# Two transformer layers on one core: GELU passes grouped on ScalarE, an earlier weight load, a new hand-made order

## The chip, the cores and the metric

The kernel runs on one core of one Trainium2 chip. A core has five engines with a queue of instructions each: TensorE (PE, matrix products), VectorE (DVE), ScalarE (ACT, table functions such as exp and GELU), GpSimd (POOL) and SyncE (SP, which here only issues DMAs). The engines run independently and wait for each other on semaphores. The metric is the device time in microseconds of one execution; the median over the runs counts.

## The reference

The input x has 2048 rows of 448. Two layers are computed, each an attention block and a mixer block:

```python
x = x + A(layernorm(x))        # attention: 16 heads of 28; softmax(q k^T / sqrt(28)) v, then @ wo
x = x + B(layernorm(x))        # mixer, on y = layernorm(x):
    h  = gelu(layernorm(y) @ w1)           # 448 -> 448
    hs = shift(h) @ w2                     # four quarters of the columns, shifted by +1, -1, +2, -2 rows
    x1 = y + hs
    B  = x1 + gelu(layernorm(x1) @ w3) @ w4   # 448 -> 1792 -> 448
```

Because the mixer shifts rows by up to two, the second half of the mixer for a tile of 128 rows needs the first half of the tile before and of the tile after.

## The kernel before, in words

The 2048 rows are 16 tiles of 128; x stays in SBUF as `x_res` for the whole kernel. Queries are worked off in units: four units of four tiles in layer 0; in layer 1 three units of four tiles and two of two (`UNITS`). Keys come in parts (`PARTS`): tiles 0 to 3, 4 to 7 and 8 to 15. `ORDER` says which unit meets which part first: in layer 0 unit 0 takes its three parts one after the other; in layer 1 units 0 and 1 alternate over the parts, so that unit 0 on the first part is followed by unit 1 on the first part. Sums of an unfinished unit are spilled to DRAM and loaded again (`t_uload`, `t_norm`).

The exponentials are the main stream. A group of two or three PSUM banks of scores (L1415) is turned into `PT` by one exp on ACT (L1458), and `PT` is multiplied with V (L1485). A share of the banks is done on DVE by a polynomial instead (`t_ditem`, L1370 to L1386). When a unit is finished its sums are copied out of PSUM (L1503), normalised, projected (`t_outproj`) and added to `x_res`.

Then the unit's mixer begins (`spawn_mixer`). `t_mixA` does the first half: statistics, `xn`, a DMA transpose, the product with w1, a copy into `hT`, and one GELU pass in place over all of it (L1648). `t_mixB` does the second half for the tiles from the one before the unit to the last but one (the last unit of layer 0 in two parts of two and three tiles): x1, `xn`, transpose, the product with w3, copies into `h2T` (L1779), two GELU passes in place over seven of 14 chunks each (L1791), and the product with w4, which ends in `x_res` (L1799). After that the next layer can take the tile: statistics, `xn` (L1052), transpose, projections to `kT`, `qT` and `vaug`. The last unit of layer 1 runs a direct variant in the tail, with a GELU per bank.

exp and GELU need different tables on ACT, and each change from one to the other inserts a table load. `GATED[L]` lists the units whose h2T passes wait until the hT pass of the next unit has been issued, so that they run under one table.

Nothing is ordered by hand in the code: every part of the work is a generator, and a planner (`Sched.run`) simulates the five engines with costs written in the code and picks the next instruction again and again. For ACT the key of a candidate is the time from which its inputs are ready; a change of table adds 1.42 us to its planned start. Ties and priorities come from latest start times of an earlier planning round, which `reorder` then shifts by the entries of a long list, `SEEDS`. The result is a fixed program for each engine's queue. When PE would be idle the planner adds filler matmuls (`keep_pe_busy`) on the tile `zero` or `ident`.

The start is in `t_setup`: the first four tiles of x go to `w4` as a staging place, the weights of the projections are loaded, statistics of four tiles are taken, one POOL instruction makes 1/sqrt(variance) for all four (`rstd`, L1156), `xn` follows, and PE transposes and projects. `t_load` issues the loads of the rest of x on POOL's queue. `t_setup2` loads the later weights (wo, w1, w3, w2, w4) once the second unit of layer 0 starts; w1 and w3 need zeroed padding first, which DVE writes (L959).

Of the kernel before, what the change touches and what calls it, by code (L numbers as in the profile page):

```python
# [8 lines left out]
ALU = mybir.AluOpType  # L9
# [168 lines left out]
class Sched:  # L178
# [174 lines left out]
    def run(self):  # L353
        P = self.P
        while True:
# [77 lines left out]
            for k, (t, choice) in enumerate(cand_list):  # L433
# [18 lines left out]
                key = (ready if eng == "act" else max(start, self.cur[eng] + self.EPS) if eng in ("pe", "dve") else start, ranks[k])  # L452
# [29 lines left out]
            if dma:  # L482
                self.cur[eng] = start + 0.1
                t_end = start + kw.get("dma_time", 3.0)
            else:
                self.cur[eng] = max(self.cur[eng], t_end)
# [109 lines left out]
def build_kernel(nc, A_x, A_wqkv, A_wo, B_x, B_w1, B_w2, B_w3, B_w4, out, n_layers=2):  # L596
# [156 lines left out]
    with st:  # L753
# [77 lines left out]
        def bi(b):  # L831
            return int(b[1:])
# [1109 lines left out]
```

## Time and profile before

| | |
|---|---|
| median of 3 runs | 1076.27 us (1075.23 to 1077.58) |
| the profiled execution: its own time, and its span | 1077.48 us, 1075.4 us |
| mean granted TensorE clock | 0.994 |
| first exp on ACT | 31.20 us |
| ACT table loads | 40 |
| exps on ACT (L1458) | 775, 881.2 us busy |
| matmuls on PE | 14185 |

The span is the time from the first to the last instruction of the profiled execution; its own time is a little longer. Times in the profile count from the span's start. Busy time is a sum over one engine; matmuls overlap, so that a busy PE is not PE at its peak. "L1458" is line 1458 of the kernel, and an arrow `out<-in` names the tiles of an instruction. "Idle before, releaser" says how long an engine stood still before an instruction and whose result it then got.

### The profile page before, as it was taken

To read this page: it belongs to the slowest core of one execution; us is meant where nothing else is said; L and a number is where in the kernel's file an instruction comes from. 1 tells how busy PE (TensorE), PEld (TensorE's weight loads), DVE (VectorE), ACT (ScalarE), POOL (GpSimd) and SP (SyncE) were. 2 spreads that over 40 slices of the span, in tenths; PEclk is the share of its full clock that TensorE was granted. 3 is DMA by queue.
4 is the path that set the end of the run, shared out by engine and by line. 5 is a ranking of instruction groups with operands and counts; after the bars stand their busy time and mean duration, and the time that the engine had idled before them with its cause. 6 is when DMAs were issued, how large, how long until landed. Compare 5 with 4: busy or idle time off the path is not lost.

```text
span 1075.4 us, 31722 instructions
## 1 busy us (share of the span) xinstructions
PE 985.7 (92%) x14185; PEld 385.1 (36%) x14188; DVE 840.6 (78%) x1855; ACT 1025.4 (95%) x924; POOL 157.1 (15%) x174
## 2 busy tenths in 40 slices
PE   5999999899999988998998999899899899999898
PEld 2333333233333333333334433333333334343455
DVE  6999999699996775756697678999998768645463
ACT  5999999799999999999999998999999999999975
POOL 4220101120111002012123012001020111110101
PEclk9999999799999999999999999999999999999999
DMA  7232105203000001000212312001111010010000
GB/s 199 60 90 63 42 2 137 55 2 36 1 21 22 1 21 22 21 7 16 61 51 66 80 46 76 21 21 41 27 15 37 2 34 12 22 39 12 20 11 23
DMA packets 77104, 41.27 MB, mean 38 GB/s; under 512 B 61288, under 2 KB 70376, under 8 KB 76968
## 3 DMA queue, kind: packets, MB, share of 16 engines
q1 hardware_dynamic: 74856, 35.58, 13.9%
q0 software_dynamic: 2112, 3.67, 1.4%
q8 instruction: 111, 1.82, 0.7%
q14 instruction: 25, 0.20, 0.1%
HBM read 14.20 MB, written 8.13 MB: 21 GB/s over the span
## 4 chain that ended last, share of the span: by engine, by line
ACT 77%; PE 18%; DVE 2%; DMA 2%; issue 1%; POOL 0%; SPq 0%; ACTq 0%; DVEq 0%
ACT PT L1458 67%; PE ps L174 8%; ACT h2T L1791 4%; PE ps L1415 4%; PE ps L1485 3%; ACT L1458 2%; DMA xT<-xn 1%; ACT hT L1648 1%; ACT L1791 1%; PE ps L1796 1%; ACT L1648 1%; PE ps L1770 1%; PE ps L1059 1%; DVE xn L1052 0%; DMA wv<-in_A_wqkv_dram 0%
## 5 line engine op out<-in xcount | busy, mean ns | idle before, releaser
L1458 ACT ACTIVATE PT<-ps 128x1536 bf16<-128x1536 f32 (+1 forms) x775 | 881.2, 1259 | 15.7 <-PE ps L1415 14.2
L1415 PE MATMUL ps<-qT,kT 32*128 32x512 bf16 (+1 forms) x2184 | 304.7, 360 | 38.5 <-ACT PT L1458 34.1
L1485 PE MATMUL ps<-PT,vaug 128*32 128x512 bf16 (+1 forms) x2184 | 232.8, 362 | 6.1 <-ACT PT L1458 4.5
L1415 PEld LDWEIGHTS ps<-qT,kT 32*128 32x128 bf16 x2184 | 76.0, 91 | 261.2 <-ACT PT L1458 149.9
L174 PE MATMUL ps<-xT,w 128*32 128x512 bf16 (+3 forms) x2412 | 159.4, 350 | 4.2 <-DMA xT<-xn 2.7
L1779 DVE CAST h2T<-ps 128x512 bf16<-128x512 f32 (+2 forms) x126 | 73.6, 584 | 37.4 <-PE ps L174 33.9
L1485 PEld LDWEIGHTS ps<-PT,vaug 128*32 128x32 bf16 x2184 | 60.6, 94 | 112.8 <-issue 52.4
L174 PE MATMUL ps<-w,h2T 128*32 128x448 bf16 x1476 | 85.9, 354 | 5.4 <-ACT h2T L1791 5.1
L1370 DVE TENSOR_SCALAR dT<-ps 128x512 f32<-128x512 f32 x116 | 79.2, 684 | 13.3 <-PE ps L1366 12.1
L174 PE MATMUL ps<-wk_pad,zero 128*32 128x256 bf16 x1796 | 84.6, 277 | 0.0
L1386 DVE SCALAR_TENSOR_TENSOR dT<-dU,dT 128x512 int32<-128x512 f32 x116 | 79.9, 689 | 0.8
L1381 DVE SCALAR_TENSOR_TENSOR dU<-dF 128x512 f32<-128x512 uint16 x116 | 79.7, 687 | 1.0
L1383 DVE SCALAR_TENSOR_TENSOR dU<-dF,dU 128x512 f32<-128x512 uint16 x116 | 79.3, 684 | 0.9
L174 PEld LDWEIGHTS ps<-xT,w 128*32 128x32 bf16 x2412 | 56.8, 95 | 62.4 <-issue 34.7
L1082 POOL TENSOR_TENSOR sq<-qT 128x512 bf16<-128x512 bf16 (+1 forms) x32 | 31.3, 985 | 264.5 <-DVE qT L1068 190.8
L1799 DVE SCALAR_TENSOR_TENSOR x_res<-x_res,mst,ps 128x448 f32<-128x448 f32 x32 | 21.5, 677 | 55.4 <-PE ps L174 44.3
L1738 POOL TENSOR_TENSOR x_res<-x_res,x1b 128x448 f32<-128x448 f32 x32 | 37.0, 1164 | 156.1 <-DVE x1b L1719 155.2
L174 PEld LDWEIGHTS ps<-wk_pad,zero 128*32 128x32 bf16 x1796 | 45.2, 96 | 24.3 <-issue 18.7
L1082 POOL TENSOR_TENSOR sq<-kT 128x512 bf16<-128x512 bf16 (+1 forms) x32 | 31.3, 980 | 130.6 <-DVE kT L1068 91.7
L174 PEld LDWEIGHTS ps<-w,h2T 128*32 128x32 bf16 x1476 | 36.5, 96 | 38.4 <-issue 10.8
L1376 DVE TENSOR_SCALAR dF<-dT 128x512 uint16<-128x512 uint16 x116 | 48.5, 418 | 0.8
L1791 ACT ACTIVATE h2T<-h2T 128x3584 bf16<-128x3584 bf16 (+2 forms) x18 | 46.9, 2605 | 1.8 <-DVE h2T L1779 1.6
(164 smaller groups left out, 1177.4 us busy)
## 6 DMA issues: line engine op xcount, KB each, us to landing
uscr<-u_sb SPq DMA_DIRECT2D x24, 256.0 KB, 2.0
uin<-uscr SPq DMA_DIRECT2D x24, 256.0 KB, 2.7
x_res<-in_A_x_dram POOLq DMA_DIRECT2D x4, 896.0 KB, 7.4
out_dram<-uin SPq DMA_DIRECT2D x16, 112.0 KB, 1.7
w<-in_B_w_dram SPq DMA_DIRECT2D x1, 1568.0 KB, 13.6
w<-in_B_w_dram SPq DMA_DIRECT2D x1, 1344.0 KB, 7.2
h2T<-in_A_wqkv_dram SPq DMA_DIRECT2D x2, 336.0 KB, 4.2
xT<-xn SPq DMA_TRANSPOSE x33, 3.7
```

Of the source, the lines that this page charges most:

```text
L174: return [self.e.matmul(out=out[c:min(c + 32, self.m)], lhsT=lhsT[:, c:min(c + 32, self.m)], rhs=rhs, start=start, stop=stop, tile_positio ...
L1082: yield op("pool", 0.1 + 0.002 * nw, lambda e, si=si: e.tensor_tensor(out=sq[:, si, 0:nw], in0=dst, in1=dst, op=ALU.mult), reads=dkeys, wr ...
L1370: yield op("dve", c_ps(cw), lambda e, b=b: e.tensor_scalar(out=dT[:, s, 0:cw], in0=ps[:, bi(b), 0:cw], scalar1=65536.0 + 127 * 128.0, scal ...
L1376: yield op("dve", c_f2b(cw), lambda e: e.tensor_scalar(out=dF[:, f, 0:cw], in0=dT[:, s, 0:cw].bitcast(U16).rearrange("p (q two) -> p q two ...
L1381: yield op("dve", c_ps(cw), lambda e: e.scalar_tensor_tensor(out=dU[:, v, 0:cw], in0=dF[:, f, 0:cw], scalar=-16384.0, in1=dF[:, f, 0:cw], ...
L1383: yield op("dve", c_ps(cw), lambda e: e.scalar_tensor_tensor(out=dU[:, v, 0:cw], in0=dF[:, f, 0:cw], scalar=EXPD * 16384.0, in1=dU[:, v, 0 ...
L1386: yield op("dve", c_ps(cw), lambda e: e.scalar_tensor_tensor(out=dT[:, s, 0:cw].bitcast(I32), in0=dU[:, v, 0:cw], scalar=EXPC * 2.0 ** -35 ...
L1415: yield op("pe", 0.012 + W / 2400.0, lambda e, bk=bk, r0=32 * j, g=g, kc=kc, q0=q0, W=W, c0=W * h: e.matmul(out=ps[:, bk, c0:c0 + W], lhsT ...
L1458: yield op("act", e_dur(n), lambda e, b0=b0, p0=p0, cnt=cnt, cw=cw: e.activation(out=PT[:, p0:p0 + cnt, 0:cw], in_=ps[:, b0:b0 + cnt, 0:cw ...
L1485: yield op("pe", 0.004 + nt * 0.0133, lambda e, j=j, rhs=rhs, vs=vs, i=i: e.matmul(out=ps[32 * j:32 * j + 32, bi(SUM), 0:128 * nt], lhsT=v ...
L1779: yield op("dve", c_ps(NW), lambda e, fch=fch, b=b: e.tensor_copy(out=h2T[:, fch, hoff:hoff + NW], in_=ps[:, bi(b), 0:NW]), reads=[("ps", ...
L1791: yield op("act", c_act(7 * NW), lambda e, f0=f0: e.activation(out=h2T[:, f0:f0 + 7, hoff:hoff + NW], in_=h2T[:, f0:f0 + 7, hoff:hoff + NW ...
```

## The change

1. In the planner, when ACT holds the GELU table, an exp is compared by its planned start, which includes the change of table, and no longer by the time it is ready. A GELU that is ready before that start goes first.
2. `GATED` of layer 0 becomes (0, 1, 2): the h2T passes of the third unit also wait for the hT pass of the fourth.
3. The zeroing of the padding of w1 and w3 moves from DVE to POOL and to the start (the one of w3 after the scratch use of that tile); the weight loads themselves stay behind the start of the second unit.
4. At the start 100 matmuls on `ident` are put on PE (`t_warm`); the first four tiles' 1/sqrt(variance) is made in two halves; and the loads of the rest of x on POOL wait for the second half.
5. In the planner a DMA issued by POOL now occupies POOL for its planned duration and not for 0.1 us.
6. `SEEDS` is another, shorter list, so that the order of all instructions changes. By the change's own words 20 table loads are left.

```diff
@@ Sched.run
-                key = (ready if eng == "act" else ...
+                key = ((start if self.act_tab == "gelu" and kw.get("tab") == "exp" else ready) if eng == "act" else ...
...
             if dma:
-                self.cur[eng] = start + 0.1
+                self.cur[eng] = start + (dur if eng == "pool" else 0.1)
@@ build_kernel
     SEEDS = [
-        (3033793134, 1, 5, -8.4), (3017015515, 1, 0, -0.6), 570578, 625884, ...
+        (3033793134, 1, 35, -35.9), 510908, 684737, (3033793134, 1, 0, -0.4), ...
     ]
-    GATED = [(0, 1), (0, 1)]
+    GATED = [(0, 1, 2), (0, 1)]
@@ t_setup
+            yield ("spawn", t_warm(), 2)
             yield ("spawn", t_load(ld_x, last), 2)
...
+        def t_warm():
+            b = yield ("acq", ["b3"])
+            for k in range(100):
+                yield op("pe", 0.06, lambda e, b=b: e.matmul(out=ps[:, bi(b), 0:128], lhsT=ident[:, :], rhs=ident[:, :], start=True, stop=True),
+                         reads=[("ident",)], writes=[("ps", bi(b))], touch=[b])
+            yield ("rel", b)
+
         def t_load(ld_x, after):
+            yield ("wait", ("rstd0",))
             for k, c in enumerate([1, 2, 3, 0]):
@@ t_setup2
+            yield op("pool", 0.5, lambda e: e.memset(w1[:, 3, :], 0.0), writes=[("w1z",), ("w1",)], nolk=1)
+            yield ("wait", ("acol",))
+            yield op("pool", 1.9, lambda e: e.memset(w3[:, 3, :], 0.0), writes=[("w3z",), ("w3",)], nolk=1)
             yield ("wait", ("segstart", first_seg[(0, 1)]))
...
-            for (dst, src_, nm, w) in ((w1, B_w1, "w1", 0.3), (w3, B_w3, "w3", 1.0)):
-                yield op("dve", w, lambda e, dst=dst: e.memset(dst[64:128, 3, :], 0.0), writes=[(nm + "z",)])
+            for (dst, src_, nm) in ((w1, B_w1, "w1"), (w3, B_w3, "w3")):
@@ new function, also called by t_ln1
+        def ln_rstd(tiles):
+            sl = slice(tiles[0], tiles[-1] + 1)
+            yield op("dve", 0.1, lambda e: e.tensor_scalar(out=vpe[:, sl], in0=mv[:, sl, 1], scalar1=EPS, scalar2=None, op0=ALU.add), ...)
+            yield op("pool", 0.4 + 0.15 * len(tiles), lambda e: e.tensor_tensor(out=rstd[:, sl], in0=vpe[:, sl], in1=neghalf[:, 0:len(tiles)], op=ALU.pow), ...)
@@ t_ln1
-            for t in tiles:
+            halves = [tiles[:2], tiles[2:]] if L == 0 and c == 0 else [tiles]
+            for part in halves[:-1]:
+                for t in part:
+                    yield from ln_stats(t, True)
+                yield from ln_rstd(part)
+            for t in halves[-1]:
...
+            yield from ln_rstd(halves[-1])
+            if L == 0 and c == 0:
+                yield ("sig", ("rstd0",))
             yield from norm_x(tiles, xs, L == 0 and c == 0)
```

More of the change, by code (lines that the diff above doesn't have):

```diff
@@ L451, in run @@
                         continue
-                key = (ready if eng == "act" else max(start, self.cur[eng] + self.EPS) if eng in ("pe", "dve") else start, ranks[k])
+                key = ((start if self.act_tab == "gelu" and kw.get("tab") == "exp" else ready) if eng == "act" else max(start, self.cur[eng] + self.EPS) if eng in ("pe", "dve") else start, ranks[k])
                 if best is None or key < best[0]:
@@ L970, in ln_stats @@
             yield op("dve", 0.2, lambda e: e.bn_aggr(out=mv[:, t, :], in_=st6[:, t, :]), reads=[("st6", t)], writes=[("mv", t)])
+        def ln_rstd(tiles):
+            sl = slice(tiles[0], tiles[-1] + 1)
+            yield op("dve", 0.1, lambda e: e.tensor_scalar(out=vpe[:, sl], in0=mv[:, sl, 1], scalar1=EPS, scalar2=None, op0=ALU.add),
+                     reads=[("mv", t) for t in tiles], writes=[("vpe", t) for t in tiles])
+            yield op("pool", 0.4 + 0.15 * len(tiles), lambda e: e.tensor_tensor(out=rstd[:, sl], in0=vpe[:, sl], in1=neghalf[:, 0:len(tiles)], op=ALU.pow),
+                     reads=[("vpe", t) for t in tiles] + [("neghalf",)], writes=[("rstd", t) for t in tiles])
         class Slot:
@@ L1152, in t_ln1 @@
             xs = yield from acq_xn(4)
-            sl = slice(t0, t0 + n)
-            yield op("dve", 0.1, lambda e: e.tensor_scalar(out=vpe[:, sl], in0=mv[:, sl, 1], scalar1=EPS, scalar2=None, op0=ALU.add),
-                     reads=[("mv", t) for t in tiles], writes=[("vpe", t) for t in tiles])
-            yield op("pool", 1.0, lambda e: e.tensor_tensor(out=rstd[:, sl], in0=vpe[:, sl], in1=neghalf[:, 0:n], op=ALU.pow),
-                     reads=[("vpe", t) for t in tiles] + [("neghalf",)], writes=[("rstd", t) for t in tiles])
+            yield from ln_rstd(halves[-1])
+            if L == 0 and c == 0:
+                yield ("sig", ("rstd0",))
             yield from norm_x(tiles, xs, L == 0 and c == 0)
```

123 rows, old and new, of the table SEEDS are left out of this document.

## The prediction

> **What bounds the kernel now.** I read the page's busy times and chain first, then the groups of ScalarE (ACT), then a table by stage. Columns of a group: busy us, mean ns of one, then idle before it.
>
> ```profile
> PE 985.7 (92%) x14185; PEld 385.1 (36%) x14188; DVE 840.6 (78%) x1855; ACT 1025.4 (95%) x924; POOL 157.1 (15%) x174
> ...
> ACT 77%; PE 18%; DVE 2%; DMA 2%; issue 1%; POOL 0%; SPq 0%; ACTq 0%; DVEq 0%
> ```
>
> ```profile
> L1458 ACT ACT_TABLE_LOAD x19 | 24.4, 1283 | 0.3
> ...
> L1791 ACT ACT_TABLE_LOAD x12 | 15.4, 1283 | 0.2
> ...
> L1648 ACT ACT_TABLE_LOAD x8 | 10.3, 1283 | 0.1
> ```
>
> ACT is busy 95% of the span and carries 77% of the chain. The three rows are its table loads: 19 back to exp, 20 to GELU; with one at the start, 40. Where is ACT not full? In the next view the fields are the stretch, its length, then busy time of PE, PEld, DVE, ACT, POOL.
>
> ```profile
> 0.00:31.20 31.20, 17.70 (x106) 8.41 (x107) 22.17 (x83) 17.73 (x27) 13.46 (x20) 1.00 0.65 173
> 31.20:186.00 154.80, 145.63 (x1885) 50.09 (x1888) 148.75 (x329) 154.71 (x139) 21.37 (x19) 1.00 0.24 63
> 186.00:216.00 30.00, 25.46 (x258) 7.83 (x251) 20.44 (x38) 23.84 (x22) 4.15 (x4) 0.77 0.35 73
> 216.00:492.00 276.00, 257.42 (x3525) 92.59 (x3527) 214.79 (x441) 275.31 (x233) 35.27 (x36) 1.00 0.09 17
> 492.00:680.00 188.00, 174.04 (x2788) 71.14 (x2780) 145.89 (x324) 179.48 (x152) 36.16 (x40) 1.00 0.22 54
> 680.00:1034.70 354.70, 329.97 (x5211) 131.26 (x5213) 268.31 (x591) 354.07 (x300) 39.38 (x46) 1.00 0.10 24
> 1034.70:1075.40 40.70, 35.45 (x443) 23.81 (x431) 20.28 (x53) 20.27 (x57) 7.27 (x10) 1.00 0.05 16
> ```
>
> ACT idles 13.5 us before the first exp, 6.2 us around 200, 8.5 us between 492 and 680, 20.4 us in the tail after the last exp, and under 1 us in each of the three long stretches: those are ACT's, and what leaves ACT there leaves the time. From 492 to 680 layer 0 hands over to layer 1. How much room PE has is shown by its filler matmuls (tile `zero`), which the planner puts in when PE has nothing to do; PE's own busy time hides that.
>
> ```profile
> 412.00:492.00 80.00, 3.20 (x84) 2.17 (x80) 0.00 (x0) 1.00 0.11 21
> 492.00:680.00 188.00, 6.02 (x132) 3.71 (x132) 0.00 (x0) 1.00 0.22 54
> ```
>
> So in those two stretches PE has 3 to 4% in reserve, and in the second one it shares the bound.
>
> **Part 1, the loads.** One GELU episode of the before, on ACT:
>
> ```profile
> 221.23 94.51 ACT L1458 ACTIVATE PT<-ps 128x1536 bf16<-128x1536 f32 x83
> 315.75 1.28 ACT L1648 ACT_TABLE_LOAD   x1
> 317.05 1.91 ACT L1648 ACTIVATE hT<-hT 112x2048 bf16<-112x2048 bf16 x1
> 318.87 2.43 ACT L1791 ACTIVATE h2T<-h2T 128x2688 bf16<-128x2688 bf16 x1
> ...
> 322.61 1.02 ACT L1458 ACTIVATE PT<-ps 128x1024 bf16<-128x1024 f32 x1
> 323.65 1.28 ACT L1791 ACT_TABLE_LOAD   x1
> 324.94 2.44 ACT L1791 ACTIVATE h2T<-h2T 128x2688 bf16<-128x2688 bf16 x1
> 327.40 1.28 ACT L1458 ACT_TABLE_LOAD   x1
> ```
>
> A single exp stands between the two halves of h2T and costs two loads. With the changed key the planner charges that exp its table switch before it compares, so the second half, ready at once, goes first. Nine pairs exist; one is together already in the tail, eight get rid of two loads each; the third unit of layer 0 joining the fourth's hT pass is two more. That makes 22 by my count; the change says 20, so one more pair of episodes must meet, which can happen where no exp is ready between them. I take 20. Price of one: neighbours under one table overlap (hT ends at 318.96, h2T starts at 318.87, 0.09), across a load they don't, and 0.02 is lost beside it (327.40 + 1.28 to the next): 1.283 + 0.09 + 0.02 = 1.39 us. Twenty are 27.8 us of ACT.
>
> [...]
>
> Ten of the twenty lie in ACT's own stretches (four in 316 to 427, four in 851 to 946, two at 996 to 1009): 13.9 us, full value at best; PE's thin reserve from 412 to 492 can eat the 2.8 us there. The other ten lie in 492 to 680.
>
> **Part 2, the hold.** Unit 2's h2T passes now wait for unit 3's hT pass. On ACT nothing queues behind them, exps pass by. But unit 2 holds tile 7, layer 1's unit 1 has tiles 4 to 7 as queries, and its exps come second in layer 1's order. The rows, DVE and ACT in order of time:
>
> ```profile
> 500.25 3.19 ACT L1791 ACTIVATE h2T<-h2T 128x3584 bf16<-128x3584 bf16 x1
> ...
> 508.39 1.78 DVE L1052 TENSOR_SCALAR xn<-x_res,mv,rstd 128x448 bf16<-128x448 f32 x4 [0.33 <-POOL rstd L1156]
> ...
> 517.96 0.69 DVE L1503 COPY u_sb<-ps 128x512 f32<-128x512 f32 x1
> ...
> 544.15 0.34 DVE L1318 TENSOR_SCALAR qT<-qT,bcol 128x512 bf16<-128x512 bf16 x1
> ...
> 562.42 1.28 ACT L1648 ACT_TABLE_LOAD   x1
> ```
>
> 517.96 is the last copy of layer 0's attention; at 544.49 unit 1's first queries are ready, just in time. In between ACT does layer 1's first unit: 64 banks, two and a half to an exp, 26 exps at 94.51/83 = 1.14 us, 29 us. Now tile 7's GELU waits for the load at 562.42, 44.5 us after the copy, where the queries were due 26.5 us after it. Two delays follow. First, exps run out until hT is ready: 0 to 44.5 - 26.5 = 18 us, as the out-projection and mixer are hurried or not. Second, from the GELU's end to the queries: 41.0 us as it ran (503.44 to 544.49, with slack in it), at the least 6.7 to the end of xn at 510.17, a transpose of 3.7 (page, row below) and about 4 of projection, 14.4. I take 4 and 19, near the low ends, because the planner sees both waits and the low ends are what the work takes; a stall of 23 us, between 14 and 59. Against it the ten loads, 13.9, and some of the old 8.5 us of idle, since PE clears its backlog in the stall: I take 6. Part 2 with its loads: 13.9 + 6 - 23 = -3 us; bounds +8 and -45.
>
> **Part 3, the weights.** The w1 and w3 pads move from DVE, where they queued behind the DVE exps, to POOL at the start; the SP DMAs that followed them can go right behind wo_pad's at 129.29, some 45 us earlier. What they collide with now:
>
> ```profile
> 129.29 2.04 SPq L956 DMA_DIRECT2D wo_pad<-in_A_wo_dram  x4
> ```
>
> ```profile
> xT<-xn SPq DMA_TRANSPOSE x33, 3.7
> ```
>
> ```profile
> 179.39 0.49 SPq L965 DMA_DIRECT2D w<-in_B_w_dram  x1
> ```
>
> ```profile
> 186.41 9.66 DMA xT<-xn
> ```
>
> ```profile
> 199.30 3.28 ACT L1458 ACTIVATE PT<-ps 128x1024 bf16<-128x1024 f32 x3 [3.79 <-PE ps L1415]
> 203.83 4.91 ACT L1458 ACTIVATE PT<-ps 128x1536 bf16<-128x1536 f32 x4 [1.25 <-PE ps L1415]
> 209.79 6.90 ACT L1458 ACTIVATE PT<-ps 128x1536 bf16<-128x1536 f32 x6 [1.05 <-PE ps L1415]
> ```
>
> The last weight load is issued at 179.39, and the transpose at 186.41 takes 9.66 us, not 3.7; PE waits, its clock falls to 0.77 of full in this stretch, ACT loses 3.79 + 1.25 + 1.05 = 6.1 us. Between 0 (another collision) and 6.1; I take 5. POOL's added memsets stand ahead of little; its x loads and squares wait 2 us at most.
>
> **Part 4, the start.** The POOL power behind the x loads, and PE before and after it speeds up:
>
> ```profile
> 7.76 0.17 DVE L1154 TENSOR_SCALAR vpe<-mv 128x4 f32<-128x4 f32 x1
> ...
> 10.90 1.08 POOL L1156 TENSOR_TENSOR rstd<-vpe,neghalf 128x4 f32<-128x4 f32 x1
> ...
> 24.45 1.03 PE L1059 MATMUL ps<-xT,wq_pad 128*128 128x512 bf16 x4
> ...
> 28.78 0.15 DVE L933 TENSOR_SCALAR sc<-sc 128x4 f32<-128x4 f32 x1
> ```
>
> ```profile
> 16.93 4.98 PE ps L1059 x12
> ```
>
> The power is ready at 7.93 and starts at 10.90: 3.0 us go when the x loads wait for it. Twelve projections take 4.98 us cold; at the later rate (1.03 for four) they take 3.1: 1.9 us go if the 100 warm-up matmuls hold. Sum 4.9; I take 5. Low end 0: the bias chain (28.78) also gates the first exp at 31.20 and may not move. High end 9: with that chain moved up too. The x loads themselves land later, but 26 exps cover them.
>
> [...]
>
> **Part 5, the order.** New seeds move everything. The tail's 41 us and the three ACT stretches may change; ACT's idle there is under 1 us each, so there is little to win and something to lose: -2, from 0 to -10 (waits such as the 1.05 and 1.25 above, a handful).
>
> **Sum.** 13.9 - 3 + 5 + 5 - 2 = 19 us off the profiled execution's 1077.48: 1058.5. That execution is 1.2 above the median of 1076.27, so about **1057**.
>
> **Rivals.** (a) Slower: the hold. If hT and the queries keep the pace they ran at, the stall is 18 + 41 = 59, part 2 is -45, the sum -23 or so: **1099**. It decides from a stall of about 42 us on. For it: both delays are in rows, and the extra pair of episodes that meets (Part 1) fits a time without exps. Against it: both paces had slack. (b) PE becomes the bound where loads go: reserve 3.20 of 80 us at 412; half of the 13.9 us is lost and the 6 us of idle stay: **1070**. For it: the filler rows. Against it: ahead of 412 and after 680 filler is plentiful. (c) The start and the weights do nothing (warm-up worn off or in front of the transposes, weights landing on another transpose): **1067**.
>
> **How the numbers follow.** Forecast 0.55, (a) 0.20, (b) 0.13, (c) 0.12. Three runs spread by 0.2%, about 2.2 us, which is what can be told from no change. The forecast itself runs from 1042 (hold at its low end, start 7) to 1068; with (b), (c) and half of (a) the range is 1041 to 1086. Faster: 0.55 + 0.25 less a little where (b) or (c) meets a longer stall, 0.77; same 0.03; slower 0.20.
>
> **What would show it.** Right: 20 loads; ACT's first exp near 26; no 3.8 us wait on ACT near 195, the weights issued near 130; one gap on ACT of 15 to 30 us between layer 1's first and second unit, ended by PE's L1415. Wrong: a gap over 40 us there, the three long stretches with several us of ACT idle, or hT of unit 3 long after the end of layer 1's first unit.

## The result, and the profile after

The changed kernel takes **1081.8 us** (median of 4, 1081.3 to 1082.66); the kernel before took 1076.92 beside it (median of 4). The ratio is **1.0048, 95% interval 1.0032 to 1.0063**: slower by about 5 us, where 19 us less were forecast. The profiled execution took 1082.12 us with a span of 1080.0; its counterpart of before 1077.48 and 1075.4. The profiles of two kernels below (b_pairs and b_hold2) fell into executions whose mean granted TensorE clock was 0.749 and 0.755, and are not read.

The page of the changed kernel, and its table loads among the groups of ACT (three more stand alone on other lines):

```profile
PE 992.2 (92%) x14226; PEld 396.8 (37%) x14229; DVE 842.2 (78%) x1857; ACT 996.5 (92%) x901; POOL 158.8 (15%) x177
...
ACT 74%; PE 18%; DVE 6%; DMA 1%; issue 1%; POOL 0%; DVEq 0%; ACTq 0%
```

```profile
L1424 ACT ACT_TABLE_LOAD x9 | 11.5, 1283 | 0.2
L1614 ACT ACT_TABLE_LOAD x8 | 10.3, 1283 | 0.1
```

So the loads did go: 20 are left, and ACT is busy 996.5 us where it was 1025.4. ACT got 29 us lighter and the kernel 5 us longer. The table by stage of the changed kernel (stretch, length, busy time of PE, PEld, DVE, ACT, POOL, granted clock) shows where ACT stood still instead:

```profile
0.00:36.10 36.10, 28.12 (x264) 18.19 (x266) 30.67 (x83) 17.29 (x25) 14.34 (x22) 0.86 0.57 149
36.10:206.00 169.90, 155.80 (x2072) 55.80 (x2075) 160.89 (x352) 168.07 (x150) 22.66 (x20) 1.00 0.28 71
206.00:335.00 129.00, 119.20 (x1572) 41.78 (x1564) 109.20 (x217) 128.95 (x113) 16.62 (x16) 1.00 0.09 13
335.00:529.90 194.90, 184.50 (x2571) 65.11 (x2571) 129.75 (x284) 192.09 (x163) 27.05 (x29) 1.00 0.10 22
529.90:576.00 46.10, 39.83 (x894) 21.88 (x890) 34.19 (x81) 15.13 (x8) 13.44 (x15) 1.00 0.21 31
576.00:669.00 93.00, 89.14 (x1310) 33.58 (x1309) 76.71 (x176) 92.58 (x81) 16.04 (x19) 1.00 0.27 74
669.00:1033.40 364.40, 334.80 (x5152) 132.64 (x5152) 275.95 (x605) 363.38 (x310) 41.53 (x46) 1.00 0.10 24
1033.40:1080.00 46.60, 40.78 (x423) 27.80 (x417) 24.85 (x66) 19.01 (x56) 7.17 (x10) 0.99 0.06 18
```

The first exp comes at 36.1 and not at 31.2; ACT is idle 31.0 of the 46.1 us from 529.9 to 576.0; the tail has 46.6 us, not 40.7. In each of the other stretches ACT stands still for 2.8 us at most.

Both kernels run 775 exps in the same sequence, so the start of the n-th exp (the first is number 0) can be laid beside its counterpart. Changes of that difference, after minus before, make the ledger:

| stretch | the exps that bound it | us |
|---|---|---|
| start | up to exp 0 | +4.9 |
| the first exps | 0 to 120 | +1.8 |
| weights | 120 to 158 | -6.2 |
| layer 0, four loads fewer | 158 to 365 | -5.3 |
| hand-over to layer 1, ten loads fewer, the hold | 365 to 485 (180.0 to 190.8 us) | +10.9 |
| layer 1, six loads fewer | 485 to the last exp's end | -7.5 |
| tail | from there to the end of the span | +5.9 |

The sum is the 4.6 us between the two profiled executions, up to rounding. The 1.8 us of the first exps are small waits for scores that the new order brings: ACT was idle for 0.09 us from 31.2 to 186.0 before, and is idle for 1.8 from 36.1 to 206.0 now.

The start, in time order (POOL, DVE and PE), and behind it the last of the four memsets as the kernel before has it:

```profile
6.39 0.71 POOL L932 TENSOR_TENSOR rstd<-vpe,neghalf 128x2 f32<-128x2 f32 x1 [4.61 <-DVE vpe L930]
...
9.09 6.02 DVE L1015 TENSOR_SCALAR xn<-w,mv,rstd 128x448 bf16<-128x448 bf16 x4
...
10.42 1.54 POOL L899 MEMSET vaug<- 128x320 bf16 x1
...
13.01 1.67 POOL L901 MEMSET wo_pad<- 128x1792 bf16 x1
...
21.13 1.91 PE L1022 MATMUL ps<-xT,wq_pad 128*128 128x512 bf16 x4 [1.11 <-DVE sc L870]
```

```profile
4.47 1.90 POOL L947 MEMSET wo_pad<- 128x1792 bf16 x1
```

The power indeed comes early (6.39 and 8.79 for the two halves, against 10.90 before). But POOL now waits 4.61 us for its operand, and four memsets that were done by 6.4 in the kernel before stand behind it; while the last two of them run, the four normalisations take 6.02 us (1.78 before). PE pauses twice meanwhile, for some 1.4 us each, its granted clock falls to 0.50 (16 to 24 us), and four projections take 1.91 us.

The hold, on ACT (L1614 is the hT pass, L1757 the h2T passes, L1424 the exps):

```profile
529.87 1.28 ACT L1614 ACT_TABLE_LOAD   x1
...
532.98 6.40 ACT L1757 ACTIVATE h2T<-h2T 128x3584 bf16<-128x3584 bf16 x2
561.38 3.43 ACT L1757 ACTIVATE h2T<-h2T 128x1792 bf16<-128x1792 bf16 x2 [22.01 <-DVE h2T L1745]
...
566.12 1.02 ACT L1424 ACTIVATE PT<-ps 128x1024 bf16<-128x1024 f32 x1
...
576.01 4.63 ACT L1424 ACTIVATE PT<-ps 128x1536 bf16<-128x1536 f32 x4 [8.87 <-PE ps L1381]
```

The two waits are 22.01 + 8.87 = 30.9 us. The extra pair of episodes that meets, which the prediction looked for, is the first part of unit 3 itself: its h2T passes at 561.38 join the held ones.

The weights, on SP's queue and on ACT, did what was forecast: the last is issued at 141.32 (179.39 before), and the waits of 3.79, 1.25 and 1.05 us near 200 are gone:

```profile
141.32 0.74 SPq L921 DMA_DIRECT2D w<-in_B_w_dram  x1
```

```profile
119.33 73.81 ACT L1424 ACTIVATE PT<-ps 128x1536 bf16<-128x1536 f32 x65
193.47 12.52 ACT L1424 ACTIVATE PT<-ps 128x1024 bf16<-128x1024 f32 x11 [0.33 <-PE ps L1381]
```

### The profile page after: what moved, and what is told of

Read it like the earlier page. It is cut to its first block, busy times and chain, and to the rows that moved or that the text cites. A ratio compares the mean times of both kernels' runs of the same rounds, so it can differ in the third digit from the quotient of the medians.

```text
span 1080.0 us, 31768 instructions
## 1 busy us (share of the span) xinstructions
PE 992.2 (92%) x14226; PEld 396.8 (37%) x14229; DVE 842.2 (78%) x1857; ACT 996.5 (92%) x901; POOL 158.8 (15%) x177
## 3 DMA queue, kind: packets, MB, share of 16 engines
q1 hardware_dynamic: 74856, 35.58, 13.9%
## 4 chain that ended last, share of the span: by engine, by line
ACT 74%; PE 18%; DVE 6%; DMA 1%; issue 1%; POOL 0%; DVEq 0%; ACTq 0%
ACT PT L1424 67%; PE ps L174 8%; PE ps L1381 4%; ACT h2T L1757 3%; PE ps L1451 2%; ACT hT L1614 1%; PE ps L1762 1%; PE ps L1736 1%; ACT L1614 1%; DVE xn L1015 1%; ACT L1424 1%; DMA xT<-xn 1%; DVE h2T L1745 1%; PE ps L1022 1%; DVE st L924 0%
## 5 line engine op out<-in xcount | busy, mean ns | idle before, releaser
L1424 ACT ACTIVATE PT<-ps 128x1536 bf16<-128x1536 f32 (+1 forms) x775 | 879.7, 1271 | 15.3 <-PE ps L1381 14.3
L174 PE MATMUL ps<-xT,w 128*32 128x512 bf16 (+4 forms) x2156 | 148.2, 352 | 3.7 <-DVE rh L1493 0.6
L1336 DVE TENSOR_SCALAR dT<-ps 128x512 f32<-128x512 f32 x116 | 79.0, 684 | 13.8 <-PE ps L1332 10.5
L174 PE MATMUL ps<-wk_pad,zero 128*32 128x256 bf16 x1856 | 89.1, 275 | 0.0
L174 PEld LDWEIGHTS ps<-xT,w 128*32 128x32 bf16 (+1 forms) x2156 | 50.2, 95 | 55.8 <-issue 25.0
L1757 ACT ACTIVATE h2T<-h2T 128x3584 bf16<-128x3584 bf16 (+2 forms) x18 | 46.9, 2605 | 22.3 <-DVE h2T L1745 22.0
L174 PEld LDWEIGHTS ps<-wk_pad,zero 128*32 128x32 bf16 x1856 | 46.6, 95 | 26.2 <-issue 21.0
L174 PEld LDWEIGHTS ps<-w,h2T 128*32 128x32 bf16 x1440 | 35.7, 96 | 40.2 <-issue 11.2
```

Of the source, the lines that this page charges most:

```text
L174: return [self.e.matmul(out=out[c:min(c + 32, self.m)], lhsT=lhsT[:, c:min(c + 32, self.m)], rhs=rhs, start=start, stop=stop, tile_positio ...
L1336: yield op("dve", c_ps(cw), lambda e, b=b: e.tensor_scalar(out=dT[:, s, 0:cw], in0=ps[:, bi(b), 0:cw], scalar1=65536.0 + 127 * 128.0, scal ...
L1424: yield op("act", e_dur(n), lambda e, b0=b0, p0=p0, cnt=cnt, cw=cw: e.activation(out=PT[:, p0:p0 + cnt, 0:cw], in_=ps[:, b0:b0 + cnt, 0:cw ...
L1757: yield op("act", c_act(7 * NW), lambda e, f0=f0: e.activation(out=h2T[:, f0:f0 + 7, hoff:hoff + NW], in_=h2T[:, f0:f0 + 7, hoff:hoff + NW ...
```

## The experiments

Two kinds of edit keep the order of everything else. One moves instructions in the finished plan: `lines(lst, n)` are all instructions that line n makes, `put(lst, ops, anchor)` puts them right behind another (`after=False`: ahead of it), and all waits are derived anew. The other alters a planner rule only in its last pass, so that due times and seeds stay and the plan is the old one up to the first decision that differs. The edits are shown shortened, with names for what the code spells out.

**The start.** a_mems moves the four memsets of the changed kernel back to the front of POOL's queue:

```diff
+        first4 = lines(lst, 897) + lines(lst, 898) + lines(lst, 899) + lines(lst, 901)
+        lst = put(lst, first4, lines(lst, 826)[-1])
```

> The changed kernel with POOL's four early memsets put ahead of the first 1/sqrt(variance), as the kernel before has them; nothing else moves. Theory POOL: DVE's four xn took 6.0 us (1.8 before) because POOL's memsets and DMA issues ran at the same time; now they take about 2 us, the first exp comes near 32 instead of 36.1, and the time falls by 3 to 4.5 us to about 1078. Rival (the cold clock of PE sets the start): xn gets faster, but the first exp stays after 35, and the time falls by under 1 us.

Measured: 1076.87, ratio to before 1.0004 (0.9995 to 1.0013): 4.9 us of the changed kernel's loss are gone by moving four memsets. Every exp comes 4.9 us earlier from number 0 on, and 5.5 to 5.6 from number 158 on. Its timeline (POOL, DVE, ACT):

```profile
4.50 1.91 POOL L901 MEMSET wo_pad<- 128x1792 bf16 x1
...
8.29 1.41 DVE L1015 TENSOR_SCALAR xn<-w,mv,rstd 128x448 bf16<-128x448 bf16 x4
...
21.80 0.21 DVE L1173 TENSOR_SCALAR bcol<-bcb,cols 128x1 f32<-128x1 bf16 x1
...
29.73 0.75 DVE L1074 SCALAR_TENSOR_TENSOR qT<-ps,sc,qT 128x512 bf16<-128x512 f32 x1
...
31.23 3.71 ACT L1424 ACTIVATE PT<-ps 128x1536 bf16<-128x1536 f32 x3 [0.98 <-PE ps L1381]
```

The four normalisations take 1.41 us again, beside three DMA issues on POOL from 8.64 on, so the loads of x alone don't hold them up; the memsets do. But the first exp is at 31.23, no earlier than in the kernel before, although the normalised x starts 3.7 us earlier and the bias (`bcol`) is there at 21.80: the last of four multiply-adds of the queries (29.73) stands late in DVE's list, which has had no pause since 23.5.

b_wp does the power alone in the kernel before (three x loads behind it), together with the early weights:

```diff
+        pw = lines(lst, 1156)[0]
+        lst = put(lst, [o for o in lines(lst, 861) if o.pos < pw.pos], pw)
+        lst = put(lst, lines(lst, 959), lines(lst, 933)[0])
+        w = lines(lst, 960) + lines(lst, 962) + lines(lst, 964) + lines(lst, 965)
+        lst = put(lst, w, lines(lst, 956)[-1])
```

> The kernel before with two edits in a fixed order: the weights' transfers right behind the output weights' (1072.6 by itself), and the three loads of x behind the first power on POOL. The prediction gave the power 3.0 us. Theory as predicted: the normalised x is ready 3 us earlier, and so is the first exp: 1069.5. Rival bias (the first exp waits for the bias chain at 28.78 and for what DVE does before it, not for the normalised x): 1072.6, and the first exp within 1 us of 31.2.

Measured: 1071.86, ratio 0.9954 (0.9942 to 0.9967); the normalised x starts at 9.22 and not at 12.03, the first exp at 31.54. The early weights have a price of their own in it, since the zeroing of the padding now stands in DVE's list ahead of the bias:

```profile
27.96 1.19 DVE L959 MEMSET w<- 64x224 uint32 x2
```

So the power is judged beside b_weights (below), which has the same two memsets and the power late: the first exp comes 0.35 us earlier (31.89 there), the whole takes 0.7 us less (1072.58). The bias chain and DVE's list gate the first exp, the low end 0 of the prediction's bounds or close to it.

a_cold takes the 100 warm-up matmuls out of a_mems:

```diff
+        w = set(map(id, lines(lst, 885)))
+        lst = [o for o in lst if id(o) not in w]
```

> The changed kernel with the four memsets moved ahead of the first power (1076.9) and without the 100 warm-up matmuls. With them the first four projections take 1.02 us, the next two sets 1.91 and 1.68, then 1.03. Theory order (the first exp at 31.2 waits for its place behind DVE's list, not for PE): the first four take 1.9, the first exp comes at most 1 us later, the whole is 1077 to 1078. Rival clock (the prediction's 1.9 us for warm projections are real and are lost again): the first exp at 33 or later, the whole 1079 or more.

Measured: 1078.49 (ratio to before 1.0017, 1.0008 to 1.0026); all exps come 1.47 us later. Neither expectation fits: the first exp is at 32.70, between them. Its PE timeline has

```profile
14.22 1.89 PE L1022 MATMUL ps<-xT,wk_pad 128*128 128x512 bf16 x4
...
17.75 1.91 PE L1022 MATMUL ps<-xT,wq_pad 128*128 128x512 bf16 x4 [1.11 <-DVE sc L870]
```

against 13.37 and 1.02 us for the first four with the warm-up. So the warm-up is worth 1.5 us in a_mems, where the normalisations start at 8.29. It was not taken out of the changed kernel with the memsets late.

**The weights.** b_weights has the last three lines of the diff above without the power:

> The kernel before, its order kept, but the two pads are written on DVE right at the start and the weight DMAs stand right behind wo_pad's on SP's queue (129 instead of 176 us). Theory collision: the transpose near 186 takes about 4 us instead of 9.7, ACT's three waits of 3.79, 1.25 and 1.05 us are gone, and the time falls by 5 to 6 us to about 1071. Rival (those waits come from the order, not from the transfer): waits and time stay within 1.5 us.

Measured: 1072.58, ratio 0.997 (0.9961 to 0.998), 4.5 us less. The padding is not zeroed at the very start, as the expectation has it, but at 28.32, ahead of the bias: the first exp comes 0.7 us later, exp 120 1.6 us later, and from there to exp 158 6.7 us are won. The waits are gone, in one run of exps without a wait from 118.68 on:

```profile
118.68 92.00 ACT L1458 ACTIVATE PT<-ps 128x1536 bf16<-128x1536 f32 x81
```

**The loads.** b_pairs moves eight exps behind the GELU passes that they stood between, on ACT alone, in the kernel before (16 loads fewer):

```diff
+        # on ACT, wherever h2T, exp, h2T or h2T, exp, hT, h2T follow each other
+        lst = put(lst, [second_h2T], first_h2T)
+        lst = put(lst, [first_h2T], hT, after=False)
```

> The kernel before, its order kept, but on ACT alone each of the eight exps that stood inside a GELU episode is moved behind it: 24 table loads instead of 40. Theory A (a load costs its 1.39 us wherever it lies): 16 x 1.39 = 22 us less, about 1054. Theory B (full price in ACT's own stretches, nothing from 492 to 680 where PE shares the bound): ten of the sixteen count, 14 us less, about 1062, and the idle of ACT between 492 and 680 grows from 8.5 to about 17 us. Theory C (holding one exp back starves PE, and the gain is lost again): less than 5 us.

Measured: 1089.13, ratio **1.012** (1.0105 to 1.0136), 12 us slower, which none of the three theories has. b_pairs2 is the same kernel once more, for its profile:

> The same kernel as the pairs run (1089.1): the kernel before with eight exps moved behind the GELU passes that they stood between, on ACT alone, 16 loads fewer. A profile to read where its 12 us go. Theory order: behind each joined pass ACT does its three ready exps and then waits some 3 to 8 us for the scores of PE, which stand in PE's list behind the w4 matmuls that wait for the second half of h2T; the sum of these waits is some 30 us against 22 us of loads and overlap. Rival tail: no such waits, and the loss comes after the last exp.

Measured: 1088.98. Waits on ACT by cause (total, times, longest), first b_pairs2, then the kernel before; and one episode of b_pairs2:

```profile
ACT PT L1458 <- PE ps L1415: 44.7, 23, 7.5
```

```profile
ACT PT L1458 <- PE ps L1415: 14.2, 14, 3.8
```

```profile
319.02 4.90 ACT L1791 ACTIVATE h2T<-h2T 128x2688 bf16<-128x2688 bf16 x2
323.94 1.28 ACT L1458 ACT_TABLE_LOAD   x1
325.23 3.28 ACT L1458 ACTIVATE PT<-ps 128x1024 bf16<-128x1024 f32 x3
333.86 1.45 ACT L1458 ACTIVATE PT<-ps 128x1536 bf16<-128x1536 f32 x1 [5.35 <-PE ps L1415]
```

Three exps were ready; for the fourth, scores are due that PE computes only after its next product with w4, as its list says. The waits grow by 30.5 us, more than 16 loads (22 us) give. Here loads saved on ACT alone were no gain.

b_key lets the planner do it: the changed key in the kernel before, in the last pass alone, without the hold (26 loads):

```diff
-                key = (ready if eng == "act" else ...
+                key = ((start if self.KEYALL and self.act_tab == "gelu" and kw.get("tab") == "exp" else ready) if eng == "act" else ...
...
+        Sched.KEYALL = True
         est, P, SC = attempt(plan)
```

> The kernel before, with the changed key in the last pass of planning alone: no hold, 26 loads in place of 40, the old seeds and the old start. Theory order (loads pay where the planner puts the other engines' work round the new places of the passes): 5 us up to exp 365 as in the changed kernel, some 8 in the hand-over, 7 in layer 1, of which the tail takes 5 back: about 1062. Rival (seeds that were chosen for the old places are worth as much as the loads; with every order kept but ACT's, 16 loads fewer cost 12 us): 1077 or more, with waits for PE's scores behind the passes.

Measured: **1068.1**, ratio 0.9926 (0.9911 to 0.9941), between the two expectations. Four loads fewer between exps 158 and 365 take 5.2 us off; the same four cost b_pairs2 7.6 us there. Four fewer in layer 1 take off 2.7 us, half their price, since ACT's idle time there grows by 1.9. Six fewer in the hand-over take off nothing: that stretch still takes 180.0 us. The other 2.4 us stand where the waits for the weights were, and chance is in them: b_key and b_kh below, with one order up to there, differ by 3.0. By stage, first b_key, then the kernel before:

```profile
475.20:655.20 180.00, 170.65 (x2717) 69.52 (x2713) 138.02 (x307) 163.47 (x137) 38.55 (x42) 1.00 0.21 57
```

```profile
482.80:662.80 180.00, 167.33 (x2666) 68.54 (x2663) 135.06 (x304) 171.47 (x144) 37.20 (x41) 1.00 0.23 57
```

ACT has 8 us less to do in the same time, and PE 3.3 us more (170.65 of 180): waits for scores (14.2 us, 7.4 before) take the place of the loads. That fits the prediction's rival (b), PE as the bound, with 2.7 us of filler left on PE; no run takes work off PE in this order to show it.

**The hold.** b_hold switches it on in the kernel before and lets the planner do all its rounds again:

```diff
-    GATED = [(0, 1), (0, 1)]
+    GATED = [(0, 1, 2), (0, 1)]
```

> The kernel before, planned again with one thing changed: the third unit of layer 0 also waits for the fourth unit's hT pass. Theory hold: layer 1's second unit gets its queries late whatever the seeds are, so ACT shows a gap of 25 to 35 us between layer 1's first and second unit, and the time is 15 to 30 us longer, about 1100 (no loads are saved to speak of). Rival (the gap in the changed kernel came from its own order): no gap over 10 us there, and a time within 8 us of 1077.

Measured: 1162.7, ratio 1.0806 (1.0792 to 1.0821), far over both expectations. 22.6 us of it are lost before the first exp already (53.76), presumably since the old seeds meet due times they were not made for. So the run doesn't price the hold; its wait is there all the same:

```profile
600.06 2.44 ACT L1791 ACTIVATE h2T<-h2T 128x2688 bf16<-128x2688 bf16 x1 [37.19 <-DVE h2T L1779]
```

To keep the rest, b_hold2 (kernel before) and b_kh (b_key) set it in the last pass alone, and a_nohold takes it out of the changed kernel in the same way:

```diff
+        GATED[0] = (0, 1, 2)      # b_hold2 and b_kh; (0, 1) in a_nohold
         est, P, SC = attempt(plan)
```

> The kernel before, with the hold of layer 0's third unit switched on in the last pass of planning alone, old key (36 loads). Order and times are those of before up to the 373rd exp; then the unit's two h2T passes go behind the fourth unit's hT at exp 409. Theory gap (a hold makes ACT wait between layer 1's first and second unit whatever the order, and the changed kernel lost its 10.9 us in the hand-over to it): one wait of 25 to 40 us on ACT after exp 409, the stretch from exp 365 to 485 goes from 180.0 to 190 or more, the whole to 1087 or more. Rival order (the hold costs nothing by itself; in the order of the changed kernel it even saves 9.5, 1081.8 against 1091.3 without it): at most 1078.

Measured: 1106.28, ratio 1.027 (1.0256 to 1.0284), 29 us slower, as the theory of the gap has it; where they go is shown by the next run.

> The kernel before with the changed key and the hold, both in the last pass of planning alone (24 loads): the run with the key by itself took 1068.1, with 180.0 from exp 365 to 485. Theory gap: one wait of 25 to 40 us after exp 409, 190 or more for the stretch, the whole 1078 or more. Rival order: at most 1069.

Measured: 1096.01, ratio 1.0173 (1.0158 to 1.0188), 27.9 more than b_key. Two waits of ACT between layer 1's first and second unit make 40.2 us:

```profile
572.63 0.20 ACT L1221 ACTIVATE fct<-dbc 128x4 f32<-128x4 f32 x1 [29.63 <-DVE dbc L1219]
...
584.35 1.45 ACT L1459 ACTIVATE PT<-ps 128x1536 bf16<-128x1536 f32 x1 [10.60 <-PE ps L1416]
```

> The changed kernel, planned again in its last pass without the hold in layer 0's third unit: the order is the same up to the 382nd exp, then the third unit's h2T passes run by themselves at 382, and two more pairs of loads come back (24 loads). From exp 365 to exp 485 the changed kernel takes 190.8 us, the kernel before 180.0. Theory H (the wait of 30.9 us on ACT is the hold's, and costs what it shows): ACT is full there, the stretch takes the 180.0 of before less six loads of 1.39, about 172, and the whole 1081.8 - 19 = 1063. Rival P (PE and DVE are what the hand-over lacks; ACT's wait only shows it in one place): waits come back in small pieces after the 382nd exp, the stretch takes 184 to 190, the whole 1075 to 1081.

Measured: **1091.26**, ratio 1.0134 (1.012 to 1.0149): without the hold the changed kernel is 9.5 us slower still. Theory H falls, and rival P priced it too low. The long wait is gone, but others come, the longest for DVE:

```profile
544.28 8.23 ACT L1424 ACTIVATE PT<-ps 128x1536 bf16<-128x1536 f32 x7 [6.48 <-PE ps L1381]
556.87 1.02 ACT L1424 ACTIVATE PT<-ps 128x1024 bf16<-128x1024 f32 x1 [4.36 <-PE ps L1381]
...
676.36 0.21 ACT L1186 ACTIVATE fct<-dbc 128x4 f32<-128x4 f32 x1 [18.69 <-DVE dbc L1184]
```

The hand-over, from exp 365 to 485, in us:

| | without the hold | with it |
|---|---|---|
| due times and seeds of before, changed key | 180.0 (b_key) | 205.5 (b_kh) |
| due times, seeds and the other edits of the changed kernel | 199.8 (a_nohold) | 190.8 (the change) |

The hold costs 25 us where the order was made without it; the changed kernel's order wins 15 of that back, and loses 20 if the hold is taken out of it. The best cell is the one that has neither.

a_less asks what makes the wait so long: it leaves out the 56 w3 steps that stand on PE ahead of unit 1's K projections:

```diff
+        w = [o for o in lst if made_by(o) == 1736][:56]   # those behind the fourth hT pass
+        s = set(map(id, w))
+        lst = [o for o in lst if id(o) not in s]
```

> The changed kernel with the 56 w3 matmul steps of layer 0's unit 3, first part, left out (that part's h2T is then not computed); every order kept. In the changed kernel they run from 551.0 to 560.6, and the K projections of unit 1 behind them from 560.65; the normalised x of that unit is ready at 549.8, a transpose takes 3.7. Theory queue (PE's list ahead of the projections makes the excess of the 36.2 us): the projections start near 554, ACT's wait of 30.9 us becomes 24 to 25, the exps after it come 6 to 7 us earlier, the whole is 1075. Rival chain (the queries wait for the normalised x, its transposes and DVE's list, and PE only fills the time): the projections start at 560 as before, the whole is 1081 to 1082.

Measured: 1083.3, ratio 1.0055 (1.0043 to 1.0067): no gain, the theory falls that these steps hold up the projections. On PE and ACT, and by stage:

```profile
559.44 5.08 PE L174 MATMUL ps<-xT,wk_pad 128*32 128x512 bf16 x48 [8.21 <-DVE h2T L1745]
```

```profile
576.93 24.18 ACT L1424 ACTIVATE PT<-ps 128x1536 bf16<-128x1536 f32 x21 [11.29 <-PE ps L1381]
```

```profile
548.00:560.00 12.00, 3.79 (x80) 1.92 (x72) 11.57 (x30) 0.12 (x1) 0.00 (x0) 0.75 0.43 89
```

PE stands still 8.21 us and still begins the projections at 559.44 (560.65 in the changed kernel): it waits for DVE's copies of h2T, and DVE is busy 11.57 of 12.0 us there. Up to the projections, DVE's list sets the pace. Behind that point it is another matter. In the changed kernel the queries are ready 14.9 us after the first projection, and in between PE also does, as its list says, a product with w4:

```profile
560.65 2.96 PE L174 MATMUL ps<-xT,wk_pad 128*32 128x512 bf16 x48
...
565.23 1.12 PE L174 MATMUL ps<-w,h2T 128*32 128x448 bf16 x20
...
567.09 1.89 PE L174 MATMUL ps<-w,h2T 128*32 128x448 bf16 x36
...
569.76 2.83 PE L174 MATMUL ps<-w,h2T 128*32 128x448 bf16 x56 [0.57 <-DVE x_res L1765]
```

These are 5.8 us, the last of them right ahead of the last projection of the queries. No run takes them out, so what PE's list costs behind 560 stays open.

**The tail.** a_oldend gives the last pass of the changed kernel the old key from 860 us on (six loads more):

```diff
-                ... kw.get("tab") == "exp" else ready) if eng == "act" ...
+                ... kw.get("tab") == "exp" and self.clock < self.KEYEND else ready) if eng == "act" ...
...
+        Sched.KEYEND = 860.0
         est, P, SC = attempt(plan)
```

> The changed kernel, with the old key in the last pass of planning from 860 us on: the order is the same up to the 711th exp, then the halves of two h2T passes and the hT pass between them stand apart again, six loads more (26). Theory PE (what ACT saves in the last 170 us comes back in the tail, since PE has 1.7 us of filler left in 163 us and begins the tail with 5.3 us more of work): the last exp ends 8.3 us later, the tail shrinks from 46.6 to about 41, the whole is 1081.8 + 2 to 3 = 1084. Rival ACT (ACT is the bound to the end and the tail's 46.6 belong to the new order): the tail stays, the whole is 1090.

Measured: 1089.54, ratio 1.0121 (1.0106 to 1.0136), 7.7 more than the change, as rival ACT has it. The last exp ends 9.3 us later and the tail shrinks by 1.7 us only, to 44.9. The tail of a_oldend, then that of b_key, which also has its passes joined:

```profile
1042.70:1087.60 44.90, 38.43 (x523) 26.12 (x519) 22.65 (x61) 19.46 (x56) 7.14 (x10) 0.99 0.04 14
```

```profile
1024.40:1065.40 41.00, 35.53 (x443) 23.87 (x435) 20.43 (x54) 20.34 (x58) 7.27 (x10) 1.00 0.05 15
```

ACT is the bound to the last exp, and six loads cost 1.5 us each there. Of the 5.9 us by which the changed kernel's tail is longer, 4.2 stay with the old key and so belong to the new order.

**Together.** b_kw is b_key with the edits of b_wp:

> The kernel before with the changed key in the last pass (1068.1 by itself) and, in that order, the weights' transfers behind the output weights' and the x loads behind the first power (1071.9 by themselves, 5.6 less than the kernel before). Theory sum (three independent gains): 1062.5. Rival overlap (the key's run already takes 3.0 us less from exp 145 to 158, where the weights' waits stood, so that much is had once only): 1065.5.

Measured: **1063.79**, ratio 0.9875 (0.9859 to 0.989): 13.8 us faster than the kernel before, 18 faster than the change. It lies between the two expectations.

## Why the prediction was wrong

**What held.** The count of 20 loads; their price in ACT's own stretches (13.9 forecast, 12.7 measured, and 1.5 each in a_oldend), though b_key's order got half of it in layer 1; the weights (5 forecast, 6.2 measured in the profiled executions, though the waits they removed differ by 3 us from run to run; 4.5 in all in b_weights); a stall of ACT between layer 1's first and second unit, of two waits, the second ended by PE's scores.

**What failed**, in us against the forecast's terms. Forecast and result lie 23.5 us apart.

- **Part 4, the start: -5 forecast, +4.9 measured at the first exp**, 9.9 of the 23.5. The step that failed is the 3.0 us for a power that no longer waits for the x loads. It counted what stood ahead of the power, and put at nothing what the earlier power leaves behind it. "POOL's added memsets stand ahead of little" (Part 3) looked at the wrong ones: the planner put the power ahead of four older memsets, and two of these then ran beside the normalisations. a_mems takes 4.9 us of it back. That still brings the first exp to 31.23 and not to 26: an earlier power gave 0.35 us there (b_wp beside b_weights). Of the 1.9 us for the warm-up, a_cold shows 1.5; in the changed kernel, with the memsets late, the first four projections took 1.89 us, where those of a_mems took 1.02.
- **Part 2, the stall: 23 forecast, 30.9 measured.** The first delay was 0, not 4: hT was ready at 529.32, and the exps ran out at 529.85. The second, from the held GELU's end (539.38) to the queries (575.53), was 36.2 and not 19; ACT filled 5.7 us of it with other work. Its three parts all came out longer than in the sum of 14.4: 10.4 to the normalised x (6.7 there), 10.9 from there to the first projection (3.7 for the transpose alone) and 14.9 from there to the queries (about 4). So the step that failed is the choice "near the low ends, because the planner sees both waits": 36.2 is near the as-run 41. What the 14.4 left out are DVE's copies of h2T ahead of the projections (a_less) and, not shown by a run, the product with w4 among them. The difference of 7.9 us is the whole miss of the hand-over (+10.9 against +3); the ten loads and the 6 us of old idle came as forecast (ACT is idle 33.4 us there, 2.5 besides the stall, where it was 8.5).
- **Part 5, the order: 2 forecast, 7.7 measured**, 1.8 in the first exps and 5.9 in the tail, of which 1.7 go with the joined passes (a_oldend). The bound of 10 held.

Rival (a), the hold, put its turning point at a stall of 42 us; with the start 9.9 and the order 5.7 us worse than forecast, 31 was enough. Its mechanism was half right: in the old order the hold does cost 27 us or more, but in the order planned for it, it is cheaper to keep than to drop. Rival (b) was priced for the wrong place: what the loads of the hand-over gave was lost again (b_key), not what those from 412 on gave. Rival (c) holds for the start, where it was too mild, and fails for the weights. What stays open: why just these due times serve the hold; no run takes the seeds apart.

The same four normalisations last 379 to 3748 ns in the changed kernel, with memsets beside them, and 394 to 483 ns in a_mems, without them (minimum, median and maximum below, in this order). The longest began at 9.40, ahead of the memset at 10.42, and ended at 13.15, 1.2 us behind the memset's end. How the memsets lengthen them, no run shows.

```profile
L1015 DVE TENSOR_SCALAR xn<-w,mv,rstd x4: 379/1066/3748, 9.1 to 14.7; 128x448 bf16<-128x448 bf16 x4
```

```profile
L1015 DVE TENSOR_SCALAR xn<-w,mv,rstd x4: 394/396/483, 8.3 to 9.2; 128x448 bf16<-128x448 bf16 x4
```

## What to carry to other kernels

In a planned order an instruction that becomes ready earlier can overtake what stood ahead of it, so ask what is now behind it and which engine that will run beside: four memsets on GpSimd, free until then, cost here about as much (4.9 us) as the four table loads saved ahead of the hand-over gave (5.3). A saving on the bounding engine counted here where the other queues were ordered anew round it, and in full only in stretches where that engine had no waits. When an order has been searched for, judge each rule with due times made for it and each order with its own rules: the hold was a loss in one order and a gain in the other, and the best kernel took the grouping, the early weights and the earlier power into the old order and left the rest.

## What the runs showed of the hardware

With the warm-up, PE's first four projections of a_mems took 1.02 us and the next four 1.91; the granted clock was 0.97 from 12 to 16 us and 0.60 from 16 to 20. From its start at 1.56 on, PE had not paused for more than 0.9 us before that fall; it was busy 2.62 of the 4 us from 12 to 16. After 8.21 us of standing still (a_less, granted clock 0.75 from 548 to 560) 48 column steps took 5.08 us, where the changed kernel's (1.00 from 548 to 560) took 2.96.
